# First token block in two halves, both gates on column tiles, and a rewritten order, in an adaLN block of windowed attention and a gMLP mixer

## The chip, the cores and the metric

The kernel runs on one core of one Trainium2 chip. The metric is the device time of one execution in microseconds, as the median of several runs. The engines are TensorE (PE), VectorE (DVE), ScalarE (ACT), GpSimd (POOL) and SyncE (SP), which only issues transfers. Each works through its own list of instructions in order, and waits on semaphores that the others raise.

## The reference

All is bfloat16: 2048 tokens of 448 features, 16 heads of 28, a causal window of 256 tokens, and a mixer of 2 x 896 hidden features that mixes over the 2048 tokens. `_layernorm` has no weights. The core of it:

```python
mod = (_silu(c) @ w_mod).reshape(c.shape[0], 6, 1, -1)
sa, ca, ga, sb, cb, gb = (mod[:, i] for i in range(6))
h = _layernorm(x) * (1 + ca) + sa
qkv = h @ wqkv                      # 16 heads of 28
scores = q k^T * 28 ** -0.5         # masked to 0 <= i - j < 256
x = x + ga * (softmax(scores) @ v) @ wo
h = _layernorm(x) * (1 + cb) + sb
z = gelu(h @ w_in)                  # 2 x 896
z1, z2 = z[..., :896], _layernorm(z[..., 896:])
g = w_sp @ z2 + b_sp                # over the 2048 tokens
x = x + gb * ((z1 * g) @ w_out)
```

## The kernel before

**Order by hand.** Nothing loops at run time. The kernel function adds some 1200 operations to a list (`sc.add`), each with the engines that could run it, its dependencies and the buffers it takes. The string ORDER (lines 19 to 74) then says in one sequence which operations run, on which engine and with which buffer slot: `671.v` is operation 671 on VectorE, `688.p.0` is operation 688 on TensorE with its first choice of PSUM banks (letters p, a, v, g, s for PE, ACT, DVE, POOL, SP). `Sched.order` (line 148) reads it, `waits` puts in the semaphore waits, `emit` writes out each engine's list. Operations that ORDER does not name are left out; `warm` (line 555) offers fillers that multiply the identity by itself, and ORDER takes 13 of them, all in the first 13 us. The durations written beside each operation were used in making ORDER; at run time they mean nothing.

**Head.** x's first 512 tokens come in two transfers of 256 tokens (`t_x0`, line 411), w_mod's first 896 columns in three pieces (`t_wmA`), the q and k columns of w_qkv in three each (`t_wq`). These are issued on SP and ACT, and x's next blocks, w_v, the rest of w_mod (`t_wmB`), w_o and w_in follow on SP. `mod_cols` (line 528) makes shift and scale of a layer norm as columns: for two vectors and four chunks of 128 features, four matmuls of one column each. The fourth chunk has 64 features; it is computed a second time into partitions 64 to 127 (line 540), because the transposed activations hold these features twice. `mod_out` brings them to `modT` in SBUF. The two gates ga and gb are rows: four matmuls each, with silu(c) repeated over 128 columns as the weights (line 570), one copy each to `gg_sb` (line 573). They scale w_o (`t_wog`, GpSimd) and w_out (`t_woutg`).

**Blocks of 512 tokens.** For each block `tb`, `stats` (line 589) takes mean and variance (VectorE) and the power -0.5 (GpSimd), `norm` writes the normalised tile `xn`. For blocks 0 and 1, PE transposes these (line 666) and the eviction applies scale and shift into `hT` (lines 678, 680); blocks 2 and 3 go through transposing transfers. Q and K of a block are eight groups of four matmuls with 512 columns. In block 0 the four groups of Q run chunk by chunk (line 696) so that they follow the evictions, then K (line 708). ScalarE or VectorE evict them to `qT` and `KT` (lines 718, 719); `q_dma` copies parts of Q to the block-diagonal `QBD`. V follows per tile (line 756).

**Attention.** Each of the 16 query tiles has two halves. A half is a score unit (32-row matmuls, line 832 or 858, and one full matmul, line 867), exponentials on ScalarE (line 819), masks on VectorE (line 874, or 894 for the first two tiles) and P times V (line 901). The score unit takes four fixed banks (0 to 3), so the next one waits for the exponential. Then a tile is divided by its sums, goes through a transposing transfer, the out-projection (line 926), the second layer norm, another transposing transfer, and the scale and shift (lines 949, 951).

**Mixer.** z2 is made per token tile (64-row matmuls, line 1011; Gelu on ScalarE, line 1018), normalised over its 896 features with two statistics and one aggregate on VectorE, the power on GpSimd and the final scaling on VectorE (line 1023). z1 is made feature by token in groups of four (line 1032). The spatial products (line 1055) are 28 groups of 16 matmuls of 512 columns, each needing all of z2; VectorE adds the bias (line 1059), GpSimd multiplies with z1 (line 1062), and four matmul groups per block give the output tiles (line 1072), with a sum (line 1082) and a store each.

Of the kernel before, what the change touches and what calls it, by code (L numbers as in the profile page):

```python
# [4 lines left out]
ACT = mybir.ActivationFunctionType  # L5
# [14 lines left out]
2.a 24.v 33.g 0.s 25.v 26.v 27.v 36.g 37.g 3.a 1.s 34.g 4.a 31.g 28.v 5.s 35.g 8.a 29.v 38.g 6.s 9.a 7.s 43.a 39.g 53.p.1 54.p.2 55.p.3 44.p.0 130.v  # L20
128.v 131.v 129.v 132.g 45.a 46.a 56.p.4 57.p.5 58.p.6 59.p.7 60.p.2 52.p.1 139.v 137.v 140.v 138.v 133.g 134.v 141.v 136.a.0 142.g 135.a.1 143.v
120.v 145.v.2 108.v 107.v 67.p.3 146.p.2 144.a.3 68.p.0 69.p.4 147.p 150.p.3 40.g 123.g 121.g 122.v 148.v 149.v 151.p 152.a 48.a 70.p.0 71.p.0
154.p.4.5.6.7 155.p 156.p 153.a 158.p 125.g 42.g 160.p 159.p 157.p 162.a 164.a 32.g 41.g 124.g 47.v 10.s 11.s 14.s 127.g 126.v 191.v 192.v 187.v 30.v
49.g 50.g 13.s 15.s 16.s 12.s 161.a 169.p.0 170.a 171.p.1 172.a 346.p.0 347.a.0 163.v 185.v 189.v 186.v 188.v 190.v 51.v 175.p.7 173.p.6 112.p.0
114.p.1 193.g 194.g 199.g 201.g 197.g 200.g.0 195.g 176.v 202.v.1 198.v.2 113.v 196.g.3 350.v 174.a 352.p.0 353.a.1 181.p.7 203.p.0 371.p.0 166.s
167.s 165.s 168.s 17.s 348.v 115.v 206.p.1 177.p.6 204.v 205.v 207.v 109.p.0 372.a.2 373.a 182.a 208.a 378.p.0 379.a.3 380.a 239.v 241.v 243.v 237.v
244.v 110.v 238.v 20.s 19.s 18.s 240.v 242.v 354.v 111.v 178.v 179.p.7 183.p.1 211.p.0 184.v 293.v 356.v 180.v 349.p.0 398.p.0 212.a 351.p 355.p
215.p.1 357.p 400.p.0 209.p.0 399.a.4.0 381.v 291.v 216.v 406.p.0 210.a 245.g 246.g 251.g 252.v.0 358.v 359.v.0 376.v 374.v 253.g 249.g 254.g.1 403.v
221.p.1 213.p.0 383.v 214.v 402.v 294.v 375.p.0 377.p 407.a.5.1 401.a 427.p.0 222.a 408.p.0 382.p 223.p.0 225.p.1 428.a.6.2 435.p.0 409.a 411.v
429.p.0 384.p 258.s 118.g 247.g 250.g.2 256.s 257.s 248.g.3 255.s 262.g 259.g 226.a 436.a.0.3 292.v 224.v 295.v 385.v 386.v.1 229.p.0 227.p.1 404.p.0  # L30
410.v 297.v 228.v 430.a 456.p.0 230.a 457.a.1.4 360.s 218.s 219.s 220.s 217.s 432.v 261.v 260.v 437.p.0 233.p.0 231.p.1 405.p 412.p 296.v 232.v 438.a
# [70 lines left out]
class Op:  # L102
    def __init__(self, n, ways, deps, prio, take, table, dma, lat, tail):
# [162 lines left out]
def bass_adaLN_cond__sliding_block__mixer_gmlp__prompt_kernel(  # L266
# [322 lines left out]
    def stats(slot, tiles, srcs, deps, prio, quick=False):  # L589
# [12 lines left out]
        if not quick:  # L602
            return rs
# [551 lines left out]
```

## Time and profile before

| what | value |
|---|---|
| median of 3 runs | 280.3 us (280.0 to 280.85) |
| the profiled execution, its own time | 279.08 us |
| its span, first to last instruction | 277.4 us |
| granted TensorE clock in the rows | 1.00 |
| first Q matmul (line 696) starts | 12.87 us |
| last z1 matmul before the spatial products | 156.5 us |
| last output matmul ends | 274.4 us |
| DMA issue to landing: x first half, second half | 3.9, 4.5 us |
| DMA issue to landing: w_mod's three first pieces | 4.4, 5.6, 5.8 us |
| DMA issue to landing: the two-chunk piece of w_q | 6.4 us |

The span is the window of one profiled execution; the time beside it also holds what lies around it. A row of the timeline gives start, length, engine, line, operation, and in square brackets how long the engine had been idle before it and what ended that. Successive instructions of one line are merged into one row (x15 is fifteen of them). A TensorE row's length includes the time in which its last matmul leaves the array, so the distance between starts says more about the rate than the length does. A few matmul records are missing.

### The profile page before, as it was taken

The numbers are of one execution on the slowest core, as the hardware profiler recorded it, in microseconds if no ns is written. First come the engines' busy times: TensorE is split into PE (matmuls) and PEld (weight loads), VectorE is DVE, ScalarE is ACT, GpSimd is POOL, SyncE is SP. The second block draws the span as 40 slices with busy tenths as digits, with TensorE's granted clock in tenths as the row PEclk, the third lists the DMA queues.
The fourth block names the chain that finished last, engine by engine and source line by source line (L and its number), as shares of the span: only waits on it lengthen the run. The fifth ranks groups of instructions, "written<-read, shape, count | busy, mean of one in ns | idle before, by whom it ended". The sixth has DMA issues, their size and how long they took to land.

```text
span 277.4 us, 7383 instructions
## 1 busy us (share of the span) xinstructions
PE 266.4 (96%) x3198; PEld 140.8 (51%) x3225; DVE 164.4 (59%) x364; ACT 128.2 (46%) x154; POOL 127.2 (46%) x191
## 2 busy tenths in 40 slices
PE   4999999999999999999999999999999999999995
PEld 1636466656576766444444444444444444444452
DVE  5679999989989999679798300300320042025434
ACT  2587999999999999577676600000000000000000
POOL 6831826914725669884949000600571065334110
PEclk9999999999999999999999999999999999999999
DMA  7966142145993666834999999100000000001113
GB/s 208 304 170 205 23 91 47 21 80 96 121 225 79 80 80 97 194 77 83 190 176 205 206 197 187 35 0 0 0 2 0 0 0 2 0 0 56 62 50 99
DMA packets 65843, 26.01 MB, mean 94 GB/s; under 512 B 56466, under 2 KB 64723, under 8 KB 65811
## 3 DMA queue, kind: packets, MB, share of 16 engines
q1 hardware_dynamic: 65168, 24.68, 43.4%
q10 hardware_dynamic: 642, 0.86, 1.1%
q8 instruction: 25, 0.41, 0.6%
q14 instruction: 8, 0.06, 0.1%
HBM read 9.01 MB, written 1.84 MB: 39 GB/s over the span
## 4 chain that ended last, share of the span: by engine, by line
PE 82%; DVE 8%; DMA 4%; POOL 3%; issue 1%; ACT 0%; ACTq 0%; SPq 0%; POOLq 0%
PE ps L1055 35%; PE ps L1032 8%; PE ps L1072 7%; PE ps L1011 6%; PE ps L708 5%; PE ps L901 5%; PE ps L858 3%; DMA hT<-xn 3%; PE ps L926 3%; PE ps L756 3%; PE ps L867 2%; DVE st_all L592 2%; PE ps L557 1%; DMA c_row<-in_c_dram 1%; PE ps L696 1%; POOL hT L951 1%
## 5 line engine op out<-in xcount | busy, mean ns | idle before, releaser
L819 ACT ACTIVATE PW<-ps 128x2048 bf16<-128x2048 f32 (+1 forms) x56 | 67.4, 1242 | 2.9 <-PE ps L867 1.1
L1059 DVE TENSOR_TENSOR tmpg<-ps,bsp_bc 128x512 bf16<-128x512 f32 x28 | 19.1, 691 | 83.4 <-PE ps L1055 69.3
L1062 POOL TENSOR_TENSOR z1T<-tmpg,z1T 128x512 bf16<-128x512 bf16 x28 | 31.9, 1153 | 79.3 <-DVE tmpg L1059 79.3
L1055 PE MATMUL ps<-wspB,z 128*128 128x512 bf16 x218 | 49.5, 379 | 0.3
L1055 PE MATMUL ps<-wspA,z 128*128 128x512 bf16 x220 | 48.8, 379 | 0.3 <-issue 0.2
L874 DVE TENSOR_TENSOR PT<-PW,mask 128x1024 bf16<-128x1024 bf16 x56 | 38.9, 721 | 0.7 <-ACT PW L819 0.7
L1055 PEld LDWEIGHTS ps<-wspA,z 128*128 128x128 bf16 x224 | 21.8, 98 | 26.6 <-issue 0.4
L1055 PEld LDWEIGHTS ps<-wspB,z 128*128 128x128 bf16 x224 | 21.9, 98 | 26.2
L600 POOL TENSOR_TENSOR rs_all<-ve_all,neghalf 128x1 f32<-128x1 f32 (+2 forms) x37 | 23.6, 645 | 3.7 <-DVE ve_all L597 3.0
L1011 PE MATMUL ps<-w_in,hT 64*128 64x448 bf16 x224 | 23.0, 349 | 1.2 <-DVE hT L951 0.6
L901 PE MATMUL ps<-Vaug,PT 128*128 128x32 bf16 x496 | 24.1, 177 | 0.1
L901 PEld LDWEIGHTS ps<-Vaug,PT 128*128 128x128 bf16 x496 | 21.8, 96 | 4.0 <-DVE PT L894 0.6
L1032 PE MATMUL ps<-hT,w_in 64*128 64x512 bf16 x196 | 22.5, 376 | 0.0
L1072 PE MATMUL ps<-w_out_g,z1T 128*128 128x448 bf16 x112 | 22.2, 352 | 0.0
L708 PE MATMUL ps<-hT,WQK 128*128 128x512 bf16 x80 | 20.5, 379 | 1.3 <-issue 0.4
L616 POOL TENSOR_SCALAR xn<-x_sb,rs_all,ve_all 128x448 bf16<-128x448 bf16 x21 | 18.1, 863 | 7.0 <-DMA hT<-xn 6.4
L901 PE MATMUL ps<-Vaug,PW 128*128 128x32 bf16 x224 | 20.1, 176 | 0.0
L592 DVE BATCH_NORM_STATS2 st_all<-x_sb 128x6 f32<-128x448 bf16 x32 | 18.9, 610 | 1.6 <-DMA x_sb<-in_A_x_dram 1.5
L592 DVE BATCH_NORM_STATS2 st_all<-z 128x6 f32<-128x448 bf16 x32 | 18.3, 607 | 1.7 <-ACT z L1018 1.7
L901 PEld LDWEIGHTS ps<-Vaug,PW 128*128 128x128 bf16 x224 | 17.6, 96 | 1.9
L597 POOL TENSOR_SCALAR ve_all<-mv_all 128x1 f32<-128x1 f32 (+2 forms) x20 | 6.6, 334 | 25.1 <-DVE mv_all L595 21.5
L1018 ACT ACTIVATE z<-ps 128x896 bf16<-128x896 f32 x16 | 14.1, 916 | 7.8 <-PE ps L1011 6.8
(101 smaller groups left out, 343.9 us busy)
## 6 DMA issues: line engine op xcount, KB each, us to landing
out_dram<-fin SPq DMA_DIRECT2D x16, 112.0 KB, 1.7
x_sb<-in_A_x_dram SPq DMA_DIRECT2D x3, 448.0 KB, 3.9
wmod<-in_w_mod_dram SPq DMA_DIRECT2D x1, 1344.0 KB, 9.5
w_in<-in_B_w_in_dram SPq DMA_DIRECT2D x1, 1344.0 KB, 8.2
QBD<-qT SPq DMA_DIRECT2D x16, 64.0 KB, 2.5
w_out_g<-in_B_w_out_dram SPq DMA_DIRECT2D x1, 784.0 KB, 4.9
bsp_bc<-in_B_b_sp_dram SPq DMA_DIRECT2D x1, 512.0 KB, 5.0
x_sb<-in_A_x_dram SPq DMA_DIRECT2D x2, 224.0 KB, 4.2
```

What stands on the lines that cost most here:

```text
L592: st = [dve(0.62 if True else 0, lambda e, t=t, ci=ci, s=s: e.bn_stats(st_all[:, slot, t, ci, :], s()), deps(t), prio) for ci, s in enumer ...
L600: rs = pool(0.53 + 0.15 * len(tiles), lambda e: e.tensor_tensor(rs_all[:, slot, a:b], ve_all[:, slot, a:b], neghalf[:, 0:b - a], ALU.pow), ...
L708: m = pe(4 * MMS, [lambda e, h=h, g=g, kc=kc, tb=tb: e.matmul(ps[:, h.slot[0], :], lhsT=WQK[:, kc, 4 * g:4 * g + 4, :].rearrange("p a b -> ...
L819: ex = act(xdur, lambda e, out_ap=out_ap, in_ap=in_ap: e.activation(out_ap(), in_ap(), ACT.Exp, scale=SCALE), [s], v - 8.0 + u, takes, tab ...
L874: return dve(0.70, lambda e: e.tensor_tensor(cols(hp.slot[0] * 2048 + 1024 * k, [[256, 4], [128, 2], [1, 128]]), cols(at_w() + 128 + 192 * ...
L901: fns.append(lambda e, hp=hp, hO=hO, hi=hi, bi=bi, kb=kb, hd=hd, nb=nb, a=at[hi][bi], p_of=p_of: e.matmul(ps[:, hO.slot[0], 32 * hd:32 * h ...
L1011: return lambda e, kc, p0, start, stop: e.matmul(ps[:, hs[t % 2].slot[hf], 0:D], lhsT=hT[p0:p0 + 64, kc, t * 128:(t + 1) * 128], rhs=w_in[ ...
L1032: return lambda e, kc, p0, start, stop: e.matmul(ps[:, hs[b // 2].slot[b % 2], :], lhsT=w_in[p0:p0 + 64, kc, ft * 128:(ft + 1) * 128], rhs ...
L1055: m = pe(16 * MMS, [lambda e, h=h, si=si, ft=ft, tb=tb: e.matmul(ps[:, h.slot[0], :], lhsT=z2[:, si, ft * 128:(ft + 1) * 128], rhs=(wspA i ...
L1059: a = dve(0.7, lambda e, h=h, ht=ht, tb=tb: e.tensor_tensor(tmpg[:, ht.slot[0], :], ps[:, h.slot[0], :], bsp_bc[:, tb * 512:(tb + 1) * 512 ...
L1062: u = pool(1.16, lambda e, ht=ht, ft=ft, tb=tb: e.tensor_tensor(z1T[tb][:, ft, :], tmpg[:, ht.slot[0], :], z1T[tb][:, ft, :], ALU.mult), [ ...
L1072: return [lambda e, ft=ft: e.matmul(ps[:, h.slot[0], 0:D], lhsT=z1T[t // 4][:, ft, (t % 4) * 128:(t % 4 + 1) * 128], rhs=w_out_g[:, ft, :] ...
```

## The change

**Block 0 in halves.** Transposes, evictions, Q and K of the first 512 tokens are made for tokens 0 to 255 and 256 to 511 separately: 8 evictions of 256 columns instead of 4 of 512, 64 matmuls of 256 columns instead of 32 of 512, 16 evictions of Q and K instead of 8. In the first half Q, then K, run chunk by chunk, each with the groups in pairs. Score units of the first tiles depend on the first half's Q (`QK_ready[...][0]`) and on K tile by tile.

**Loads.** ScalarE issues c and w_mod's large piece. SP issues x's first half, the two other pieces of w_mod, w_q's three, then x's second half, w_k's three, x's block 1. w_modB also waits for the first column matmuls.

**Columns and gates.** `mod_cols` computes the fourth chunk once with 128 columns instead of twice with 64; the 64 that spill over are zeros (`t_p2b`) for the first pair, and for the second pair one transfer (`d_modB`) copies partitions 0 to 63 of two columns of `modT` to 64 to 127, for which the columns are rotated by one. The gates are computed with 64-column weights, ga on partitions 0 to 63 and gb on 64 to 127 of one bank; one copy, then three transfers (`d_gg0`, `d_gg1`, `d_gg2`) spread each over 128 partitions.

**Normalisation.** `stats` now makes the shift (minus mean times power) for all its tiles in one operation, where `norm` had one GpSimd operation per tile. For the odd tiles of z2 (BY_ACT) the Gelu also sums its row, a Square on ScalarE gives the sum of squares, three small operations give variance and power. Tiles 0, 4, 8, 12 (BY_POOL) keep the statistics but are scaled on GpSimd.

**Output.** Tile 15 is made, summed and stored in two halves of 224 columns.

**ORDER** is new throughout. Decoded, what it says around these places:

- PE, head, before: 3 fillers, silu columns, 5 fillers, columns, filler, 4 transposes, 2 fillers, 12 transposes, 2 fillers, Q, two K groups, score unit 0.0, two K groups, gate 0, gate 1, score unit 0.1, V tile 2, ...
- PE, head, after: 2 fillers, silu columns, 5 fillers, columns, 8 transposes, 2 fillers, Q chunk 0, filler, rest of Q's first half, K's first half, 8 transposes, score unit 0.0, Q's second half, one K group, score unit 0.1, three K groups, score unit 1.0, gates, second columns, V tile 1, ...
- ACT, head, after: norm of tile 1, two evictions, pads of q and k, three Q evictions, norm of tile 3, three K evictions, one eviction of the second half, first exponential, three Q evictions, exponential.
- DVE, head, after: ... norm of tile 0, pad, clear of QBD, modT, two evictions, statistics of tiles 3 and 2, two pads, shift, norm of tile 2, one Q and one K eviction, three evictions of the second half, statistics of block 1.
- Out-projections start behind the score units of tile 9, before: of tile 6. 13 of h2's 16 scalings are on VectorE (before 4), 2 on ScalarE (5), 1 on GpSimd (7).
- POOL, end of z2, after: power of tile 15, power of tile 14, scaling of tile 0, shift, scaling of tile 12, scaling of tile 8, then the spatial products' multiplications. PE's list ends with the products of tiles 15 (halves), 12, 14, 13 and 1.

```diff
-    t_x0 = [load("d_x0%d" % i, "sp", 0.25, ..., prio=-98.99 + 0.001 * i, land=(2.9, 3.4)[i]) for i in range(2)]
+    t_x0 = [x_half("sp", 0, -98.99, 2.9, 2.9), x_half("sp", 1, -98.935, 8.0, 3.5)]
...
-    t_screp = dve(0.5, lambda e: e.tensor_copy(sc_rep[:], sc_sb[:].unsqueeze(2).broadcast_to([128, DC, 128])), [t_sc, t_x[1]], -16.0)
+    t_screp = dve(0.5, lambda e: e.tensor_copy(sc_rep[:], sc_sb[:].unsqueeze(2).broadcast_to([128, DC, 64])), [t_sc, t_x[1]], -16.0)
...
-                m = 128 if ch < 3 else 64
+                m = 128 if ch < 3 or not bank_col else 64
...
-    t_mA = pe(1.2, mod_cols(hA, (0, 1), True), [t_wmA, t_sc, t_p2], -60.0, [hA])
+    t_mA = pe(0.92, mod_cols(hA, (0, 1), False), [t_wmA, t_sc, t_p2, t_p2b], -60.0, [hA])
+    for d in t_wmB:
+        d.deps.add(t_mA)
...
+    t_modB.append(add({"sp": (0.6, lambda e: e.dma_start(modT[64:128, 11:13], modT[0:64, 11:13]))}, list(t_modB), -14.9, dma="d_modB", lat=0.05, tail=2.0))
+    hG = Hold(bM)
+    t_gate = pe(0.78, [lambda e, kc=kc, v=v, p0=p0: e.matmul(
+        ps[p0:p0 + 64, hG.slot[0], 0:D], lhsT=sc_rep[:, kc, :], rhs=wmod[:, kc, v * D:(v + 1) * D],
+        start=(kc == 0), stop=(kc == DC - 1), tile_position=(0, p0)) for kc in range(DC) for v, p0 in ((2, 0), (5, 64))],
+                [t_wmB, t_screp, t_p2], -14.0, [hG], "cols64")
+    t_graw = dve(0.7, lambda e: e.tensor_copy(gg_sb[:, 0, :], ps[:, hG.slot[0], 0:D]), [t_gate], -14.0)
...
+    t_gup = [spread("d_gg%d" % k, lambda p=p: gg_sb[p:p + 64, 1, :], lambda: gg_sb[64:128, 0, :], [t_graw]) for k, p in enumerate((0, 64))]
+    t_gg = [[t_graw, spread("d_gg2", lambda: gg_sb[64:128, 0, :], lambda: gg_sb[0:64, 0, :], [t_graw, t_gup])], t_gup]
...
+        by = lambda e: e.scalar_tensor_tensor(ve_all[:, slot, a:b], mv_all[:, slot, a:b, 0], -1.0, rs_all[:, slot, a:b], ALU.mult, ALU.mult)
...
-        nm = pool(0.34, lambda e: e.tensor_scalar(ve, m, z, -1.0, ALU.mult, ALU.mult), deps, prio)
...
+        for hf in range(2 if tb == 0 else 0):
+            xl = [xs[2 * hf], xs[2 * hf + 1]]
...
+                    four = range(4 * qk, 4 * qk + 4)
...
+                if hf == 0:
+                    for kc in range(DC - 1):
+                        for n in range(2):
+                            pair = four[2 * n:2 * n + 2]
...
+                        last[g] = pe(4 * MMH, [part(g, kc, hq[g], hf) for kc in range(DC)], [evh[hf], t_wqk[qk]], vv + 0.001 * g, [hq[g]])
...
+    BY_POOL = (0, 4, 8, 12)
+    BY_ACT = (1, 3, 5, 7, 9, 11, 13, 15)
...
+            g = act(1.1, lambda e, to=to, of=of, total=total: e.activation(to(), of(), ACT.Gelu_apprx_tanh, accum_out=total), need, v, table="gelu")
...
+            q = act(1.1, lambda e, t=t, less=less, square=square, hj=hj: e.activation(
+                fin[:, 2 * hj.slot[0]:2 * hj.slot[0] + 2, :].rearrange("p a d -> p (a d)"), z2[:, t, :], ACT.Square, bias=less, accum_out=square), [a], v, [hj])
...
+            r = pool(0.6, lambda e, t=t: e.tensor_tensor(rs_all[:, 2, t:t + 1], ve_all[:, 2, t:t + 1], neghalf[:, 0:1], ALU.pow), [b, t_nh], v - 0.01)
...
+            for c0, c1 in ((0, D // 2), (D // 2, D)) if t == NT - 1 else ((0, D),):
```

More of the change, by code (lines that the diff above doesn't have):

```diff
@@ L121, in __init__ @@
         self.land = None
+        self.least = 1.0
 class Sched:
@@ L179, in order @@
             if op.land is not None:
-                op.end = max(at + 1.0, op.land)
+                op.end = max(at + op.least, op.land)
                 dma_at = max(dma_at, op.end - 2.0)
```

356 lines of the change are left out of this document (214 added, 142 removed).

## The prediction

> **What bounds the kernel now.** I read the page first (shares of engines, then the chain of waits).
>
> ```profile
> span 277.4 us, 7383 instructions
> ...
> PE 266.4 (96%) x3198; PEld 140.8 (51%) x3225; DVE 164.4 (59%) x364; ACT 128.2 (46%) x154; POOL 127.2 (46%) x191
> ...
> PE 82%; DVE 8%; DMA 4%; POOL 3%; issue 1%; ACT 0%; ACTq 0%; SPq 0%; POOLq 0%
> ```
>
> TensorE is the bound: its work can only start earlier, shrink, or be stalled less. Each record holds some 0.17 us of pipeline, so I took the spacing of starts from the timeline: 512 columns cost 0.2156 us, 448 cost 0.189, 128 cost 0.056 (sixteen L743 matmuls in 0.89 us). Summing these over the matmuls and subtracting from the timeline leaves the true stalls: the head up to 12.87 us, 0.85 us at 18 us, about 1.1 us between 29 and 37 us, 1.75 us between 109 and 117 us. Almost none from 120 us to the last matmul at 274.4; then 2.95 us for the last sum and store. The head:
>
> ```profile
> 5.68 2.32 PE L557 MATMUL ps<-ident 128*128 128x512 bf16 x5
> ...
> 10.10 1.06 PE L557 MATMUL ps<-ident 128*128 128x512 bf16 x2
> 10.95 1.43 PE L666 MATMUL ps<-ident,xn 128*128 128x128 bf16 x12
> 12.22 0.59 PE L557 MATMUL ps<-ident 128*128 128x512 bf16 x2
> 12.87 3.40 PE L696 MATMUL ps<-hT,WQK 128*128 128x512 bf16 x15
> ...
> 18.68 0.29 PE L832 MATMUL ps<-qT,KT 32*128 32x128 bf16 x8 [0.69 <-ACT KT L718]
> ...
> 20.64 1.68 PE L570 MATMUL ps<-wmod,sc_rep 128*128 128x448 bf16 x8
> ```
>
> L557 only keeps the array busy; useful work starts at 12.87. The spacing matters too: two L557 from 10.10 to 10.95 are 0.43 us each and the transposes 0.107, twice the later figures, though PEclk reads 1.00. Full speed comes near 12.6 us, 3.4 us after the unbroken stretch that began at 9.27.
>
> Then windows, for the end of attention and what follows:
>
> ```profile
> 110.00:115.00 5.00, 4.61 (x58) 2.21 (x54) 3.08 (x9) 2.17 (x2) 4.12 (x9) 1.00 0.60 119
> 115.00:120.00 5.00, 4.44 (x48) 2.10 (x46) 4.58 (x12) 3.34 (x4) 4.24 (x9) 1.00 0.93 216
> 120.00:125.00 5.00, 5.00 (x48) 2.23 (x46) 3.62 (x12) 3.88 (x5) 4.01 (x9) 1.00 0.32 64
> ```
>
> (window, PE, PEld, DVE, ACT, POOL, clock, DMA.) The stall of 109 to 117 is here; VectorE and GpSimd are busy, ScalarE has room.
>
> **Part 1, the head.** I walked the new ORDER engine by engine with durations of this trace. x's first half keeps its issue, 0.79, and its landing 3.9 later: statistics from 4.76, two of 0.58, two aggregates 0.30, variance 0.17, GpSimd's power 0.73, shift 0.16, then two norms side by side (ScalarE 0.75): 8.2. w_mod landed at 7.6 (SP's third issue, 1.8, plus 5.8) behind all of x and beside w_q; now it is done with 1.0 MB moved instead of 1.23. x's second half landed at 5.8 with 0.93 MB moved, so between the two: estimate 6.2. Its 64 column matmuls, not 80, at 18 ns (80 took 1.44) end by 7.5. Eight transposes at 0.107 end at 9.1, two fillers at 9.97. VectorE meanwhile does a pad 0.28, the 0.91 clearing of QBD (L521), modT 0.30 and the first eviction 0.33 (from 0.54 for twice the columns): 9.7. So Q starts at 10.0, not 12.87.
>
> It does not keep those 2.9 us. Until about 11.65 (8.25 + 3.4) a 256-column matmul costs 0.213, then 0.109; with one filler of 0.43 Q ends at 12.8, K at 14.6. x's second half, moved behind w_q, has 1.62 MB ahead; w_q's large piece landed at 8.8 (2.4 + 6.4) with as much, so 8.8. VectorE takes it at 9.95: 1.16 + 0.30 + 0.17, GpSimd 0.73, and one norm at 12.9; but the other norm stands on ScalarE behind three Q evictions that need Q's last matmul (three of 0.39, estimated from L718's 0.60 and L819's 1.03 for 512 and 1024 columns): 14.75. Transposes to 15.25; ScalarE has three K evictions before its share of the next: 16.15. Second halves of Q and K, 32 x 0.109, and one score unit 0.25: 20.05. Score unit three needs the exponential of unit two, which follows a table load of 1.28: done at 20.75. Before, the same work ended at 20.65 plus two units of 0.22 still to come: 21.1. **Head: -0.35 us.** Its ends: -2.9 if nothing is late after the early start, +2.3 if the array stays slow one more 3.4 us stretch (rival 1).
>
> The issues: ScalarE's queue has two, not five, SP gets the rest, one per 0.5 to 0.6 us; the last w_k piece goes out near 6.6, not 4.8, but its turn by bytes is 10, and its pads are needed at 12.8. w_modB now waits for the first column matmuls, whose own load it already waited for: no later than 8.7.
>
> **Part 2, gates and columns.** Eight gate matmuls take 1.51 us (20.81 to 22.32). On two column tiles four pairs cost 4 x 0.189 = 0.76, plus a switch of shape, for which the nearest row is L832: eight 128-column matmuls on four row tiles should take 0.11 and take 0.23, so 0.12. **-0.63 us**; bounds +0.12 (pairs do not overlap) and -0.75. [...] The second set of columns loses 16 of 80 matmuls at 15 ns: **-0.24**.
> One copy of 0.62 remains of two on VectorE. Four new transfers (modT, three for gates) take 4 x 0.6 us on SP, which was idle from 22.8 to 31.2. They land 2.5 after issue (QBD's row), the last in a chain of two at about 28.4; the first reader, wo_g on GpSimd, started at 31.2. Without that cover GpSimd would stand there us for us, and block 3's norms behind it. x's last block, queued behind the wait for the gate copy, leaves at 23.4 instead of 22.3, lands by 28.7, and is read near 32.
>
> **Part 3, normalisation.** Twelve GpSimd shifts for blocks 1 to 3 (L614, 0.48 mean) become three VectorE ones of 0.16. Of z2's sixteen tiles, eight lose two statistics and an aggregate, 8 x 1.40 = 11.2 us of VectorE, and gain on ScalarE a Square and an accumulator each: 0.92 (L1018) to 1.2 (448 columns from SBUF take 0.75, scaled), some 8.5 us. ScalarE had 16 us idle from 110 to 157, so this hides, and is worth 8.5 us of PSUM waits if it did not. Four tiles' final scaling goes to GpSimd. With h2's scalings moved from GpSimd to VectorE and out-projections kept back as filler, I give back **1.0** of the 1.75 us stall (bounds -1.75, and +4.3, rival 2), and **0.5** of the 1.1 between 29 and 37 (0 to -1.1), where the first exponential is 2.5 us earlier.
>
> **Part 4, at nothing.** The last tile in halves: in the new ORDER tile 1, whole, is the last product, so the 2.95 us tail stays; were tile 15 last, half of 0.62 would go. 512 as 256-column matmuls: 32 more at 2.3 ns, 0.07. The shared shape of spatial products is untouched.
>
> **Sum**: -0.35 - 0.63 - 0.24 - 0.5 - 1.0 = -2.7. The profiled execution took 279.08 (span 277.4): 276.4. The median of three is 280.3, 1.2 above; the same step from it gives **277.6 us**.
>
> **Rivals.**
> 1. *The array stays slow.* PE pauses between the columns and the transposes (7.5 to 8.25) and there are three fewer fillers. If full speed came one stretch later, 16.0, Q and K's first halves would cost 32 x 0.213 + 0.43 = 7.3 us, ending at 17.2 instead of 14.6: +2.6, in all **280.2**, no change. [...] Against: from 8.25 the order is unbroken. [...]
> 2. *GpSimd holds the spatial products* (slower). They need all sixteen z2 tiles; GpSimd's queue ends with power, tile 0, a shift, tile 12, tile 8. After the last z2 matmul PE has four z1 groups, 112 x 0.108 = 12.1 us. ScalarE's last Square ends some 5 us in, small operations take 2, leaving 5.1 for three scalings. The row below (L951's) is 512 columns at 0.76 to 1.79; 896 columns are 1.33 to 3.14, three 4.0 to 9.4. At the slow end PE stands 4.3 us: **281.9**. It delays from 1.7 each and makes the kernel slower from 2.9 each. For: GpSimd slows beside a busy VectorE. Against: the median is 767.
>
> ```profile
> L951 POOL TENSOR_SCALAR hT<-hT,modT x7: 762/767/1793, 100.4 to 131.6; 128x512 bf16<-128x512 bf16 x7
> ```
>
> 3. *The early start carries through.* -2.9, both stalls fully gone (-2.85) and part 2: -6.6, **273.7**. For: ScalarE and TensorE both get the score chain sooner. Against: the walk above ends at ScalarE.
> 4. *Halves do not pay at all* (x's second half lands near 11): head +1.1, rest as forecast: 279.0, inside the forecast's range.
>
> **Chances.** Forecast with 4: 0.57; rival 1: 0.13; rival 2: 0.13; rival 3: 0.17. About 0.3%, 279.5 to 281.1, is what a measurement of this kernel can tell from no change. Faster 0.73 (forecast but 0.03, rival 3, a little of rival 1), same 0.12, slower 0.15 (rival 2, and rival 1 with one more stall). The range 274.2 to 280.8 leaves out rival 2 and rival 3's end; the forecast alone is 275.8 to 279.4.
>
> **What would show it.** First useful Q matmul near 10 us; QK's last near 20; the gate's eight matmuls within 0.9 us; spacing 0.213 then 0.109 inside Q's first half; the wait of ScalarE's second norm on PE; no PE gap before the first spatial product; gaps of 109 to 117 halved. Wrong: QK still ending after 21, or a PE gap over 1 us near 152.

## The result and the profile after

The changed kernel takes 280.94 us (median of 20 executions, 280.01 to 282.97); the kernel before, on the same chip, 279.95 (20 executions, 278.2 to 282.4). The ratio is 1.0055, 95% interval 1.0034 to 1.0076: about half a per cent **slower**, where 277.6 and "faster" had been forecast, and just above the range. The profiled execution has a span of 279.0 us against 277.4.

From the page of the changed kernel, the lines that answer to those shown of before, and the row of the granted clock over the 40 slices:

```profile
span 279.0 us, 7462 instructions
...
PE 266.4 (96%) x3222; PEld 143.8 (52%) x3245; DVE 160.2 (57%) x373; ACT 133.0 (48%) x179; POOL 117.1 (42%) x174
...
PEclk9999999999999999979999999999999999999999
...
PE 71%; POOL 13%; DVE 8%; issue 4%; DMA 2%; ACT 0%; SPq 0%; POOLq 0%
```

TensorE's busy time has not changed by a tenth; VectorE and GpSimd do less, ScalarE more. GpSimd has gone from 3% to 13% of the chain that ends last, DMA stands at 2%, and one slice of the clock, the 18th (119 to 126 us), reads 7.

TensorE's timeline at the head:

```profile
8.71 1.06 PE L747 MATMUL ps<-hT,WQK 128*128 128x256 bf16 x4
9.57 0.63 PE L569 MATMUL ps<-ident 128*128 128x512 bf16 x1
9.99 3.27 PE L747 MATMUL ps<-hT,WQK 128*128 128x256 bf16 x28
...
14.95 2.36 PE L747 MATMUL ps<-hT,WQK 128*128 128x256 bf16 x20 [0.65 <-DVE hT L708]
...
18.88 0.40 PE L907 MATMUL ps<-qT,KT 32*128 32x128 bf16 x16
19.21 0.95 PE L582 MATMUL ps<-wmod,sc_rep 128*64 128x448 bf16 x8
20.09 0.95 PE L544 MATMUL ps<-sc_sb,wmod 128*128 128x1 bf16 x32
20.91 0.92 PE L831 MATMUL ps<-wv,hT 128*128 128x448 bf16 x4
```

The head is better than forecast. Q starts at 8.71 us, Q, K and three score units of the first block are done at 19.2, the gates take 0.88 us from start to start. The same work, counted as in the prediction, ended in the kernel before at 21.1, and with gates and second columns at about 23.8: a lead of 1.9 us, then of 2.9. This is one execution. In the eleven profiled executions with this order of loads (the changed kernel and all runs below but e7 and e8) the gates start between 19.2 and 20.3 us, so a lead read from one profile is uncertain by about a microsecond.

The loss is behind 105 us. TensorE there, and the same stretch in windows of one us (PE, PEld, DVE, ACT, POOL, clock, DMA):

```profile
107.18 1.69 PE L1089 MATMUL ps<-w_in,hT 64*128 64x448 bf16 x16 [0.29 <-DVE st_all L612]
...
112.36 2.82 PE L1089 MATMUL ps<-w_in,hT 64*128 64x448 bf16 x28
115.47 0.92 PE L1001 MATMUL ps<-wo_g,hT 128*128 128x448 bf16 x4 [0.28 <-DMA hT<-o_sb]
118.37 0.93 PE L1001 MATMUL ps<-wo_g,hT 128*128 128x448 bf16 x4 [1.99 <-DMA hT<-o_sb]
119.24 7.15 PE L1089 MATMUL ps<-w_in,hT 64*128 64x448 bf16 x56
...
158.29 4.05 PE L1158 MATMUL ps<-wspA,z 128*128 128x512 bf16 x18 [0.16 <-issue]
```

```profile
119.00:120.00 1.00, 1.00 (x8) 0.34 (x8) 1.00 (x3) 0.84 (x2) 0.30 (x1) 0.65 0.21 29
120.00:121.00 1.00, 1.00 (x8) 0.39 (x6) 0.97 (x2) 0.00 (x0) 0.85 (x3) 0.50 0.64 148
121.00:122.00 1.00, 1.00 (x8) 0.46 (x6) 0.96 (x5) 0.67 (x1) 0.42 (x3) 0.50 1.07 369
122.00:123.00 1.00, 1.00 (x8) 0.41 (x6) 0.96 (x4) 0.46 (x2) 0.38 (x2) 0.64 1.22 344
123.00:124.00 1.00, 1.00 (x14) 0.53 (x12) 0.88 (x3) 0.00 (x0) 0.90 (x2) 1.00 1.39 210
```

The output product of block 15 (omm.j15, 118.37) waits 1.99 us for its transposed attention output, and behind this pause 8 matmuls a microsecond run instead of 14: 3.4 us (0.7 x 1, 2 x 1, 0.7 x 1) at half the clock, worth some 1.7 us. TensorE is never idle in the windows from 119 to 123; "PE 1.00" hides the loss, and only the clock column and the counts show it.

Why the transposed rows are late is seen on SP's queue, which issues the transposes in order, and on GpSimd:

```profile
105.64 1.26 SPq L475 DMA_TRANSPOSE hT<-o_sb  x1
109.39 3.41 SPq L475 DMA_TRANSPOSE hT<-xn  x2
112.84 1.27 SPq L475 DMA_TRANSPOSE hT<-o_sb  x1
114.57 1.19 SPq L475 DMA_TRANSPOSE hT<-xn  x1
115.82 1.25 SPq L475 DMA_TRANSPOSE hT<-o_sb  x1
```

```profile
107.31 1.86 POOL L637 TENSOR_SCALAR xn<-x_sb,rs_all,ve_all 128x448 bf16<-128x448 bf16 x1
...
112.80 0.71 POOL L637 TENSOR_SCALAR xn<-x_sb,rs_all,ve_all 128x448 bf16<-128x448 bf16 x1 [2.21 <-DMA hT<-xn]
```

Block 14's attention output was ready at 106, but its transpose (112.84) stands behind those of h2 blocks 5 and 4 (109.39), which waited for a GpSimd norm that took 1.86 us (107.31) where its shortest took 0.71. From 106.9 to 109.4 SP issues nothing; then five transposes of 1.2 to 1.7 us each are due at nearly the same time, and block 15's is the last of them.

How much this stage costs can be summed. Its two ends in the kernel before:

```profile
109.32 2.25 PE L1011 MATMUL ps<-w_in,hT 64*128 64x448 bf16 x22 [0.29 <-ACT PW L819]
...
156.59 3.62 PE L1055 MATMUL ps<-wspA,z 128*128 128x512 bf16 x16 [0.16 <-issue]
```

From the first z2 matmul to the first spatial product TensorE has 224 x 0.0945 + 196 x 0.108 + 4 x 0.756 + 0.6 (the last PV) = 46.0 us of work (45.2 in the kernel before, where one output product is already done). It took 51.1 us (107.18 to 158.29) against 47.3 (109.32 to 156.59): **5.1 us lost, where 2.1 were lost before**. Of the 3.0 us between them, 1.3 are longer waits (0.28 and 1.99, against 0.40 and 0.56) and 1.7 are the half clock. At the stage's start the lead is still 1.3 us; 1.6 of the 2.9 had gone on the way. Two of the waits on the way are large, and the second is taken up by e4:

```profile
38.85 0.19 PE L976 MATMUL ps<-Vaug,PT 128*128 128x32 bf16 x1 [0.59 <-DVE o_sb L992]
...
46.82 0.81 PE L789 MATMUL ps<-hT,WQK 128*128 128x512 bf16 x3 [1.32 <-DVE Vaug L836]
```

### The profile page after: what moved, and what is told of

It reads as the page before. It is cut to its first block, busy times and chain, and to the rows that moved or that the text cites. A ratio compares the mean times of both kernels' runs of the same rounds, so it can differ in the third digit from the quotient of the medians.

```text
span 279.0 us, 7462 instructions
## 1 busy us (share of the span) xinstructions
PE 266.4 (96%) x3222; PEld 143.8 (52%) x3245; DVE 160.2 (57%) x373; ACT 133.0 (48%) x179; POOL 117.1 (42%) x174
## 4 chain that ended last, share of the span: by engine, by line
PE 71%; POOL 13%; DVE 8%; issue 4%; DMA 2%; ACT 0%; SPq 0%; POOLq 0%
PE ps L1158 34%; PE ps L1177 8%; PE ps L1135 8%; PE ps L1089 6%; POOL xn L637 5%; PE ps L789 4%; POOL rs_all L620 3%; PE ps L976 2%; PE ps L831 2%; PE ps L933 2%; POOL ve_all L627 1%; PE ps L747 1%; DVE PT L949 1%; DVE st_all L612 1%; DMA hT<-xn 1%
## 5 line engine op out<-in xcount | busy, mean ns | idle before, releaser
L949 DVE TENSOR_TENSOR PT<-PW,mask 128x1024 bf16<-128x1024 bf16 x56 | 37.9, 709 | 1.7 <-ACT PW L894 1.7
L620 POOL TENSOR_TENSOR rs_all<-ve_all,neghalf 128x1 f32<-128x1 f32 (+2 forms) x29 | 19.4, 672 | 12.3 <-DVE ve_all L617 7.0
L1089 PE MATMUL ps<-w_in,hT 64*128 64x448 bf16 x224 | 23.9, 368 | 0.3 <-DVE st_all L612 0.3
L637 POOL TENSOR_SCALAR xn<-x_sb,rs_all,ve_all 128x448 bf16<-128x448 bf16 x22 | 20.6, 939 | 5.5 <-DMA hT<-xn 3.7
L617 POOL TENSOR_SCALAR ve_all<-mv_all 128x1 f32<-128x1 f32 (+1 forms) x16 | 4.7, 295 | 42.4 <-DVE mv_all L615 41.3
L1177 PE MATMUL ps<-w_out_g,z1T 128*128 128x448 bf16 (+1 forms) x119 | 22.0, 341 | 0.0
L1135 PE MATMUL ps<-hT,w_in 64*128 64x512 bf16 x196 | 21.6, 376 | 0.0
L789 PE MATMUL ps<-hT,WQK 128*128 128x512 bf16 x68 | 17.8, 379 | 2.1 <-DVE Vaug L836 1.3
L1187 DVE TENSOR_TENSOR fin<-ps,x_sb 128x448 bf16<-128x448 f32 (+1 forms) x17 | 9.8, 593 | 14.9 <-PE ps L1177 14.8
L1089 PEld LDWEIGHTS ps<-w_in,hT 64*128 64x128 bf16 x224 | 11.2, 98 | 11.9 <-issue 2.3
```

The source lines that it names most:

```text
L620: rs = pool(0.53 + 0.15 * len(tiles), lambda e: e.tensor_tensor(rs_all[:, slot, a:b], ve_all[:, slot, a:b], neghalf[:, 0:b - a], ALU.pow), ...
L637: op = add({"dve": (0.42, on_dve), "pool": (0.75, lambda e: e.tensor_scalar(to[:, h.slot[0], 0:D], x_sb[:, t, :], z, ve, ALU.mult, ALU.add ...
L789: m = pe(4 * MMS, [lambda e, h=h, g=g, kc=kc, tb=tb: e.matmul(ps[:, h.slot[0], :], lhsT=WQK[:, kc, 4 * g:4 * g + 4, :].rearrange("p a b -> ...
L949: return dve(0.70, lambda e: e.tensor_tensor(cols(hp.slot[0] * 2048 + 1024 * k, [[256, 4], [128, 2], [1, 128]]), cols(at_w() + 128 + 192 * ...
L1089: return lambda e, kc, p0, start, stop: e.matmul(ps[:, hs[t % 2].slot[hf], 0:D], lhsT=hT[p0:p0 + 64, kc, t * 128:(t + 1) * 128], rhs=w_in[ ...
L1135: return lambda e, kc, p0, start, stop: e.matmul(ps[:, hs[b // 2].slot[b % 2], :], lhsT=w_in[p0:p0 + 64, kc, ft * 128:(ft + 1) * 128], rhs ...
```

## The experiments

Kernels are compared by their ratio to the kernel before, timed on the same chip beside them. "Lost" is the excess over 46.0 us (45.2 for "before" and e7, which have the old order) in the profiled execution, as above; "half rate" counts the timed executions whose mean granted clock was 0.994 or less (one stretch of 3.4 us at half rate lowers the mean of 279 us by 0.006); "pause" is TensorE's longest recorded wait of the profiled execution between 107 and 135 us. The pause belongs to one execution of each kernel, the half rate to all of them.

| kernel | ratio [95%] | lost, us | pause, us | half rate |
|---|---|---|---|---|
| before | 1 | 2.1 | 0.56 | 6 of 105 |
| changed | 1.0055 [1.0034, 1.0076] | 5.1 | 1.99 | 17 of 20 |
| e1_oT_first | 1.0051 [1.0019, 1.0084] | 3.0 | 1.90 | 9 of 12 |
| e2_fill_gap | 1.0005 [0.9977, 1.0033] | 3.8 | 0.41 and fillers | 0 of 12 |
| e4_h1_gpsimd | 1.0021 [0.9994, 1.0048] | 3.5 | 2.26 | 6 of 12 |
| e5_ready_work | 0.9991 [0.9961, 1.0021] | 3.4 | 1.77 | 2 of 12 |
| e6_ready_h1 | 1.0022 [0.9989, 1.0055] | 3.7 | 1.77 | 0 of 12 |
| e7_pause_before | 1.0028 [0.9998, 1.0057] | 1.4 | 0.58 | 1 of 12 |
| e8_x_whole | 1.0096 [1.0061, 1.0131] | 5.7 | 2.74 | 6 of 6 |
| e9_five_xn | 1.0065 [1.0041, 1.0089] | 5.4 | 2.28 | 9 of 12 |
| e12_all_four | 0.9986 [0.9962, 1.0010] | 2.6 | 1.06 | 3 of 12 |
| e13_all_five | 0.9979 [0.9959, 0.9999] | 3.1 | 1.06 | 2 of 12 |
| e14_gates_row | 1.0064 [1.0042, 1.0086] | 5.1 | 2.01 | 7 of 11 |
| e15_all_six | 0.9943 [0.9919, 0.9966] | 1.4 | 0.34 | 0 of 8 |

In the diffs a line of ORDER is written with the names of its operations, one engine at a time.

**e1_oT_first.** The two late transposes move forward in SP's queue: block 14's ahead of those of h2 blocks 5 and 4, block 15's ahead of block 4's.

```diff
 SP:
-oT.j13 h2T.j5 h2T.j4 oT.j14 h2T.j6 oT.j15 h2T.j8
+oT.j13 oT.j14 h2T.j5 oT.j15 h2T.j4 h2T.j6 h2T.j8
```

> The changed kernel with SyncE's queue alone reordered: the transposing transfers of attention tiles 14 and 15 go ahead of second-norm transfers that wait for GpSimd. My theory (late transfers stop TensorE for 2.3 us near 116 us, and the pause halves its rate from 119.3 to 122.6 us, another 1.65 us): both out-projections find their tile, no gap over 0.5 us there, clock 1.00 throughout, 3 to 4 us less than the changed kernel, so about 277 us, 0.985 to 0.993 of before. Rival A (the head start was used up before 107 us and the pause only shows it; the work behind it waits anyway, for the second norms): the gap moves behind the out-projections, less than 1 us won.

The output products run without a wait, and TensorE then stands for h2 instead:

```profile
115.20 1.69 PE L1001 MATMUL ps<-wo_g,hT 128*128 128x448 bf16 x8
118.79 5.54 PE L1089 MATMUL ps<-w_in,hT 64*128 64x448 bf16 x56 [1.90 <-DVE hT L1026]
```

The wait has changed its name and kept its place and length. In this run SP's order decides which of the transposes is late, not that one is. The profiled execution happens to be one without half rate (span 276.9); 9 of the 12 timed ones have it, some of them twice, and the median does not gain, where 3 to 4 us had been expected. One profile would have told the wrong story here.

**e2_fill_gap.** Ten more of the matmuls that only keep the array busy (L569) ahead of omm.j15.

```diff
 PE:
-omm.j14 omm.j15
+omm.j14 warm40.3 warm40.4 warm40.5 warm40.6 warm40.7 warm40.8 warm40.9 warm40.10 warm40.11 warm40.12 omm.j15
```

> The changed kernel with ten identity matmuls of 512 columns (2.16 us) on TensorE between the last two out-projections; the transfer is as late as before. My theory (the half rate comes from the pause): clock 1.00 throughout, the pause is filled but not shortened, 1.3 to 1.8 us less than the changed kernel. Rival B (the half rate is not tied to the pause): a stretch of half rate remains and the time is equal or up to 0.5 us longer.

No execution of the 12 is at half rate any more, and the ratio falls from 1.0055 to 1.0005: some 1.4 us (0.4 to 2.4 by the two intervals) for matmuls that compute nothing, while omm.j15 comes no earlier (119.88). So the half-rate stretch is caused by TensorE standing still there, and is about 1.4 us of the loss; the waiting itself is still there, as filler.

**e4_h1_gpsimd.** Aims at the wait of 1.32 us ahead of 46.82, where four modulations of h1 in a row on VectorE stand before a V eviction, while GpSimd is idle.

```diff
 GpSimd:
-wog2 wog0 rs0.t12
+wog2 wog0 h1mod.b2.ch2 h1mod.b2.ch3 rs0.t12
 VectorE:
-h1mod.b2.ch2 h1mod.b2.ch3
```

> The changed kernel with two of the four scalings of block 2 moved from VectorE, where all four ran from 43.6 to 46.0 us, to GpSimd, idle from 36.2 to 41.5 us. My theory (the head start of 2.9 us at 21 us is partly lost because VectorE is late at 45 us): the TensorE gap of 1.3 us near 45 us shrinks below 0.5, but the time changes by less than 0.7 us, since the pause at 116 us is set by GpSimd and SyncE. Rival A (everything before 107 us counts): about 1 us less than the changed kernel.

The wait falls to 0.36, with another of 0.20 just ahead of it. How much of this arrives at 107 us can be read by the distance from the first gate matmul to the first z2 matmul, which leaves out how late the head was: 87.97 us in the changed kernel and 88.06 to 88.17 in the six other runs of the changed kernel without this edit (e1, e2, e5, e8, e9, e14), 87.37 here and 87.36 to 87.58 in the four others that have it (e6, e12, e13, e15). So some 0.6 us of the 1.6 lost between 21 and 107 come back. What that is worth at the end is not shown: the ratio 1.0021 is lower than the changed kernel's, but the intervals overlap, and half rate is also rarer here (6 of 12).

**e8_x_whole.** Undoes the move of x's second half.

```diff
 SP:
-ld x0.0 ld wmAb ld wmAc ld wqb ld wqa ld wqc ld x0.1
+ld x0.0 ld x0.1 ld wmAb ld wmAc ld wqb ld wqa ld wqc
```

> The changed kernel with the second half of x's first 512 tokens loaded right behind the first half again, ahead of the w_mod and w_q loads; nothing is left out. It undoes the part of the head that my prediction put at 0.35 us. Theory A (the start of the Q products is set by w_mod's and w_q's arrival, which the second half of x delays): the first Q matmul comes 0.7 to 1.0 us later than 8.7, the lead over the kernel before at the end of the first block's K products falls by as much, and as the pause near 116 us follows the rest of the kernel, the time is 281.3 to 282. Rival (the pause near 116 us is set by transfers and norms that do not follow the head): the time stays at 280.9, only the pause gets shorter.

Q starts at 9.69 instead of 8.71, the gates at 21.23 instead of 19.21, the first z2 matmul at 109.40 instead of 107.18, and the ratio is 1.0096, 0.41% or 1.1 us above the changed kernel; with six executions and overlapping intervals, that size is uncertain by about as much. The gates come 0.9 to 2.0 us later than in the eleven executions of the other order (19.2 to 20.3). A late head is carried through attention: its sixteen blocks, under one order, come later by what the head is late (the reciprocals of blocks 0 to 15 stand 2.0 to 2.2 us later throughout).

**e14_gates_row.** Four gate matmuls of one column tile, then four of the other.

```diff
-        start=(kc == 0), stop=(kc == DC - 1), tile_position=(0, p0)) for kc in range(DC) for v, p0 in ((2, 0), (5, 64))],
+        start=(kc == 0), stop=(kc == DC - 1), tile_position=(0, p0)) for v, p0 in ((2, 0), (5, 64)) for kc in range(DC)],
```

> The changed kernel with the eight gate matmuls in the order of the two gates, four of one column tile and then four of the other, instead of turn by turn; nothing is left out. It undoes the overlap of the two column tiles, which my prediction put at 0.63 us. If the two tiles run side by side only when they alternate, the eight take 1.5 us instead of 0.8 at 19.2 us, and what is lost at the head reaches the end as with e8_x_whole (1.2 us for 2 us): 281.2 to 281.7. Rival (two tiles overlap in any order, or the loss is covered behind 21 us): 280.9 as before.

```profile
19.70 0.96 PE L582 MATMUL ps<-wmod,sc_rep 128*64 128x448 bf16 x8
20.59 0.95 PE L544 MATMUL ps<-sc_sb,wmod 128*128 128x1 bf16 x32
```

0.89 us from start to start against 0.88: the order of the two tiles does not matter, and the time is the changed kernel's within the intervals. The overlap of the two tiles stayed, so this run does not show what the gates are worth at the end.

**e7_pause_before.** Meant to build the pause into the kernel before. (A first form of this, e3_before_late_oT, with block 15's transpose moved three places back on SP, gave no time.)

```diff
 SP:
-oT.j15 h2T.j10 h2T.j11 h2T.j8
+h2T.j10 h2T.j11 oT.j15 h2T.j8
 PE:
-z2mm.t4.3 z1mm.1.0 omm.j15
+z2mm.t4.3 omm.j15 z1mm.1.0
```

> The kernel BEFORE with the pause built in: on SP's queue the transposes h2T.j10 and h2T.j11 ahead of oT.j15, and on TensorE omm.j15 ahead of z1mm.1.0 instead of behind it; nothing is left out. Theory A (a pause of about 2 us in a full-rate stretch is enough for a half-rate stretch behind it, whatever the head does): oT.j15 is issued near 120.5 us and lands near 123, TensorE pauses about 2 us ahead of omm.j15 near 121, most executions show a mean granted clock of 0.994 or less, and the time rises by 2 us of pause and about 1 us of half rate, to 282.5 to 284. Rival (the half rate belongs to the changed kernel, to its column tiles or its denser start, not to the pause): the clock stays at 1.000 and only the pause is paid, 281.5 to 282.5.

The pause did not come: the whole of attention ran later in the profiled execution, and omm.j15 waited 0.58 us. So it does not test what it was for. But that execution is one of the few of the old order at 0.994, and its trace shows where:

```profile
72.39 0.38 PE L867 MATMUL ps<-QBD,KT 128*128 128x512 bf16 x1 [1.08 <-DMA QBD<-qT]
...
72.91 2.95 PE L756 MATMUL ps<-wv,hT 128*128 128x448 bf16 x8
```

```profile
73.00:74.00 1.00, 1.00 (x7) 0.40 (x4) 0.90 (x3) 0.00 (x0) 0.72 (x1) 0.57 0.52 65
74.00:75.00 1.00, 1.00 (x4) 0.38 (x3) 0.45 (x2) 0.59 (x2) 0.00 (x0) 0.50 0.93 234
75.00:76.00 1.00, 1.00 (x15) 0.27 (x17) 0.10 (x1) 0.44 (x1) 0.00 (x0) 0.50 2.42 91
76.00:77.00 1.00, 1.00 (x39) 0.66 (x32) 1.00 (x5) 0.35 (x1) 0.00 (x0) 0.72 0.21 14
```

A late transfer of QBD leaves TensorE idle for 1.08 us, and from 73.1 to 76.6 us 3.4 us at half rate follow. It needs neither the change's order nor its column tiles.

**e9_five_xn.** GpSimd's wait of 2.21 us at 112.80 is for a buffer: three hold the second norm's rows, and each is free only when its transpose has landed. Here there are five, taken in turn.

```diff
-    xn2, xn2_off, _ = alloc("xn2", [128, 3, DP], BF16)
+    xn2, xn2_off, _ = alloc("xn2", [128, 5, DP], BF16)
-    x2R = Res(range(3), [(i,) for i in range(3)])
+    x2R = Res(range(5), [(i,) for i in range(5)])
```

> The changed kernel with five buffers for the second norm's rows (xn2) instead of three, taken in turn; no instruction moves and nothing is left out. Theory A (the stage behind 105 us is a ring: GpSimd's norm waits for a buffer, the buffer for its transpose, the transpose for its place in SP's queue): GpSimd's waits for a transpose at 112.8, 117.3 and 119.7 us (2.2, 0.25 and 1.2 us) go, and the h2 of blocks 8 to 11 comes some 2 us earlier; but oT.j14 still stands behind h2T.j5 and h2T.j4 on SP, so the pause near 116 us stays at 1.5 to 2 us, and the time falls by less than 0.5 us: 280.4 to 280.9. Rival (the buffers are the bound of the whole stage, the pause too): 278.5 to 279.5, clock 1.000.

GpSimd's waits for buffers shrink from three (3.7 us) to one of 1.14, and the pause stays, 2.28 us. The buffers are not what makes the pause; that rival falls.

**e5_ready_work.** Puts useful work that is ready, a group of value products on h2 of blocks 0 to 3, into the pause, as the kernel before had it; the PSUM banks of the products behind it change with the order.

```diff
 PE:
-omm.j14 omm.j15 z2mm.t6.. z2mm.t4.. z1mm.1.. z1mm.0.. z2mm.t10.0 z2mm.t8.0
+omm.j14 z1mm.0.. omm.j15 z2mm.t6.. z2mm.t4.. z1mm.1.. z2mm.t8.0 z2mm.t10.0
 ScalarE:
-z2gelu.t3 z2sq.t3 z2gelu.t4
+z2gelu.t3 z1gelu.b0.f0 z1gelu.b0.f1 z1gelu.b0.f2 z1gelu.b0.f3 z2sq.t3 z2gelu.t4
```

> The changed kernel with the first group of value products, z1mm.0 (28 matmuls that need only the first four blocks' h2), between the output products of blocks 14 and 15, the eight z2 products of blocks 4 to 7 after it, and its four Gelus ahead of z2gelu.t4; nothing is left out. Theory A (the time is lost where TensorE pauses near 116 us, in two parts: the pause of 2.0 to 2.3 us itself and, in most executions, about 3.3 us at half rate behind it): the pause falls under 0.5 us, no execution shows a mean granted clock of 0.994 or less, and the time falls by 2 to 3 us from the changed kernel's 280.9, to 278 to 279. Theory B (only the half rate costs; what pauses is on a chain of norms and transfers that sets the end by itself): as with the ten filler matmuls, 280.2, with the pause turning up again at the next z2 products. Theory C (the lead is lost somewhere behind 126 us): 280.9 as before.

Theory B came true in its time (0.9991) and in the place where the wait turns up again; its reason, a chain of norms and transfers, did not hold, as e6 and e12 show. The pause at 116 is gone (0.25), and 1.77 us come back at 131.6, at the z2 products of blocks 8 to 11. **e6_ready_h1** adds e4's edit.

> The kernel of e5_ready_work with two of the four first-block-2 modulations (chunks 2 and 3 of h1mod of tokens 1024 to 1535) moved from VectorE to GpSimd, as in e4_h1_gpsimd; nothing is left out. Theory A: the 1.48 us pause at 45 us falls to about 0.5, and since the pause near 116 us is now covered, that microsecond reaches the end: 0.5 to 1 us below e5_ready_work, 277.3 to 278.3. Theory B: no gain over e5_ready_work, since the norms near 107 us, not TensorE, set the time there.

The first z2 matmul comes 1.6 us earlier than in e5 (0.9 of it is the earlier head of that execution, 0.7 e4's edit), and the end is no better (1.0022, an interval that holds 1 and e5's ratio): what is gained ahead stops at the same wait. VectorE's timeline in e6 says whose it is:

```profile
127.75 0.15 DVE L1116 TENSOR_SCALAR mv_all<-st_all 128x1 f32<-128x1 f32 x1 [1.99 <-ACT z L1112]
...
128.44 0.40 DVE L1026 TENSOR_SCALAR hT<-hT,modT 128x512 bf16<-128x512 bf16 x1
```

VectorE stands 1.99 us in front of a 0.15 us mean of tile 5 (z2mean.t5), which needs ScalarE's Gelu of that tile, now the last of four; h2's modulations, which TensorE waits for, stand behind it. With that mean moved behind them (e12), this wait is gone.

**e12_all_four, e13_all_five, e15_all_six.** e12 is e6 with e1's SP order and with z2mean.t5 behind those modulations; e13 adds the five buffers; e15 lets the next z2 products take the PSUM banks that come free first.

```diff
 VectorE (e12):
-z2mean.t5 xnc1.t13 bn2.t0.1 h2mod.b2.ch2 xn1.t14 ag2.t0 h2mod.b2.ch0 h2mod.b2.ch1 xnc1.t14 h2mod.b2.ch3
+xnc1.t13 bn2.t0.1 h2mod.b2.ch2 xn1.t14 ag2.t0 h2mod.b2.ch0 h2mod.b2.ch1 xnc1.t14 h2mod.b2.ch3 z2mean.t5
 ScalarE (e15):
-z1gelu.b0.f5 z1gelu.b0.f6 z2sq.t5 z1gelu.b0.f4 z1gelu.b1.f0
+z1gelu.b0.f4 z1gelu.b0.f5 z1gelu.b0.f6 z1gelu.b1.f0 z2sq.t5
```

> e6_ready_h1 with two more moves, nothing left out: on SP oT.j14 and oT.j15 ahead of h2T.j5 and h2T.j4 (as in e1_oT_first), and on VectorE z2mean.t5, which waited 2.0 us for ScalarE's eighth Gelu, behind the four h2mod of blocks 8 to 11 that stood behind it. Theory A (what is left in e6_ready_h1 is the pause of 1.77 us at 128 us, and that is VectorE's order): the pause at 128 us falls under 0.7 us, those near 116 stay under 0.7, no half rate: 277.3 to 278.3 with the kernel before at 279.8. Rival (the ring of norms, buffers and transposes sets the end): the pause turns up at the next z2 products and the time stays at 279 to 279.6.

> e12_all_four with five buffers for the second norm's rows instead of three; nothing left out. Theory A: 0 to 0.4 us below e12_all_four. Rival (the ring): 1 us or more below it, 277.5 to 278.3.

> e13_all_five with the pair of PSUM banks of the z2 products of blocks 9 and 11 exchanged and ScalarE's four value Gelus of that group ahead of z2sq.t5, so that the ninth block's z2 products take the banks that come free first; nothing left out. Theory A (TensorE's wait of 1.06 us for a value Gelu at 131 us, the last pause over 0.5 us behind 107 us, is on the path to the end): the wait goes, the time falls by 0.5 to 1 us below e13_all_five, to 0.993 to 0.996 of the kernel before. Rival (behind it the next norms or Gelus are as late): the wait moves on by one group, 0.997 to 0.999.

e12 comes to 0.9986, where 0.991 to 0.995 had been expected, and e13 to 0.9979. Each still has a wait of 1.06 us near 131, for a value Gelu; in e12:

```profile
131.64 2.63 PE L1089 MATMUL ps<-w_in,hT 64*128 64x448 bf16 x26 [1.06 <-ACT z1T L1143]
```

That they beat the changed kernel is plain; that the buffers add anything is not (the intervals overlap). In e15 the last wait is gone:

```profile
113.10 2.82 PE L1089 MATMUL ps<-w_in,hT 64*128 64x448 bf16 x28
115.85 0.93 PE L1001 MATMUL ps<-wo_g,hT 128*128 128x448 bf16 x4
116.71 3.20 PE L1135 MATMUL ps<-hT,w_in 64*128 64x512 bf16 x28
119.84 0.93 PE L1001 MATMUL ps<-wo_g,hT 128*128 128x448 bf16 x4
120.88 5.68 PE L1089 MATMUL ps<-w_in,hT 64*128 64x448 bf16 x56
126.40 3.19 PE L1135 MATMUL ps<-hT,w_in 64*128 64x512 bf16 x28
129.54 5.47 PE L1089 MATMUL ps<-w_in,hT 64*128 64x448 bf16 x56
```

No line ends in a wait. The stage loses 1.4 us, no execution is at half rate, and the kernel takes 277.81 us (277.43 to 278.80, 8 executions) against 279.41 of the kernel before: **0.9943, faster than both kernels**. It does all of the change; what differs is only the order behind 30 us, two operations moved to GpSimd, the PSUM banks of some products and two more buffers. Of the runs only this one, with all the edits together, is plainly faster than the kernel before (e13's interval ends at 0.9999); which of them could be left out, no run shows.

## Why the prediction was wrong

The sum had five terms. Three were right in sign, and together larger than forecast; two had the wrong sign, and they decide.

- **Part 1, the head, -0.35: mechanism right, size wrong.** The lead is 1.9 us at 19.2 in this execution, 0.8 to 1.9 in the eleven (against the one trace of the kernel before). The first mis-sized term is the landing of x's first half, kept at 3.9 us: VectorE takes it at 3.60 without a wait, so it landed at most 2.8 us after its issue. Its statistics start there, not at 4.76, so Q starts at 8.71, not 10.0; K's first half ends at 13.3, not 14.6; and the second half's transposes start at 13.29, not 14.75. Of the waits I had named, the one for the second half's norm does not show; 0.65 for its modulation does, a microsecond or more earlier than forecast. Full rate came at 9.99 in this execution (0.215 spacing before it, 0.11 after), not at 11.65 and not one stretch later, so rival 1 did not happen. The 8.25 + 3.4 behind 11.65 was my estimate from one stretch of the kernel before (9.27 to 12.6), though rows of TensorE run without a recorded wait from 5.38 there, and no run shows it to hold: here full rate comes 2.95 us behind the first transpose (7.04), and in e6 and e14 the transposes at 7.34 and 7.69 have it already (0.056 and 0.055 each).
- **Part 2, -0.63 and -0.24: right.** Gates 0.88 us instead of 1.51; with the columns the lead grows from 1.9 to 2.9, so that 0.37 is left for them.
- **Part 3, "0.5 of the 1.1 between 29 and 37": wrong sign.** TensorE waits 0.59 us at 38 for an attention output on VectorE and 1.32 at 45 for a V eviction behind four modulations. Between 21 and 107 us the lead falls from 2.9 to 1.3; e4 shows that the second of these waits is the order's, and that some 0.6 us can be had back. The rest was not tried.
- **Part 3, "I give back 1.0 of the 1.75 us stall": the step that failed.** The stage lost 5.1 us instead of 2.1, so the term was +3.0, not -1.0; it lies within the bound (+4.3) that I had written beside it and then put at GpSimd's last operations. With the terms as they turned out, -1.9 - 0.63 - 0.37 + 1.6 + 3.0 = +1.7, the span's +1.6.

Neither sign that I had named for being wrong appeared (QK ended at 19.2, no gap near 152); what failed is "gaps of 109 to 117 halved".

The step counted on the out-projections that the new order keeps back as filler. They were no filler, because they were not ready: omm.j14 and omm.j15 are the products that wait for their transposes (0.28 and 1.99 us). What the step left out is of two kinds. First, I argued from the busy shares of engines (VectorE and GpSimd full, ScalarE with room) and walked ScalarE's, VectorE's and GpSimd's order at the head, but never SP's order behind 105 us: oT.j14 behind two transposes whose rows a GpSimd norm delivers last. And the new order finishes attention earlier (block 15's reciprocal at 109.6, not 113.9) and keeps its z1 products for later, so where the old order had z1 work in front of omm.j15, the new one has nothing that is ready. e5 shows that this work, put back in its place, removes the wait there, and e15 that the time falls below both kernels once the next two waits go as well. Second, a pause has a price beyond its length: half the clock for 3.4 us in 17 of 20 executions, about 1.4 us by e2.

Rival 2 (GpSimd ahead of the spatial products) did not come: the first spatial product starts after 0.16 us of issue. A slow GpSimd norm does matter, but some 50 us earlier, as the one that holds SP's queue back at 107 to 109 us. Rival 3's condition, an early start that carries, is seen within attention (e8) and, in part, at the end of e15.

What stays open: e15 still gives back part of its lead between 21 and 107 us, and no run separates what the halved x, the gates and the columns are each worth at the end in a kernel without the pause.

## What to carry to other kernels

A gain at the head is worth what the first stage with little ready work lets through: sum that stage's matmuls and compare with its length, before and after, and walk the in-order queue that feeds it, the DMA issuer's too. When a wait is removed and the time stands still, look for a wait of like length under another name downstream (here omm.j15, then h2 of blocks 4 to 7, then 8 to 11, then a PSUM bank), and remove the row of them before judging the idea. Read the clock of every execution beside its time: a profile may be the one execution without the loss.

## What the runs showed of the hardware

**Behind a pause of about 2 us most executions ran some 3.4 us at half rate.** Kernels whose profiled execution shows a pause of 1.9 to 2.3 us had a mean clock of 0.994 or less in 48 of 67 executions (changed, e1, e4, e9, e14), with 2.74 us (e8) in 6 of 6, with 1.77 as the longest (e5, e6) in 2 of 24, with 1.06 (e12, e13) in 5 of 24, and e15, without one, in 0 of 8. The changed order without e4's edit also waits 1.3 us at 45, and e2, where that is the longest, shows none. Where the stretch lies is seen in the profiled executions alone: in the changed kernel, e8, e9 and e14 it begins between 0.2 us before and 1.5 us behind the pause's end, and in e7 behind a pause of only 1.08 us. In the changed kernel it is 3.4 us long (119.3 to 122.7). Much the same pause sometimes costs nothing (1.90 us in e1's profiled execution, 2.26 in e4's, both at clock 1.00 throughout).

**The order of the matmuls of two column tiles did not matter**: eight in 0.88 us taking turns, 0.89 four and four.

**A VectorE norm of 0.40 us took 1.69** (11.46 us, while GpSimd cleared a buffer), and GpSimd norms of 0.71 took up to 2.11. The slow one of 1.86 at 107.31, while VectorE was masking (L949), set SP's queue back at 109 us. In the kernel before, a GpSimd modulation (L951) took 1.79 us at 106.67, where VectorE ran two masks (L874, 106.69 to 107.98), against a median of 0.77; the one ahead of it, beside a division on VectorE (L917, 106.15), was over in 0.75 to 0.77. That the other engine is the cause was not tested.

**ScalarE's sums along a row are an instruction of their own**, 0.18 to 0.24 us behind each Gelu and Square that has one; sixteen of them are 3.3 us of ScalarE beside 8.4 for the eight Squares. Part 3's 8.5 us fits the Squares alone. ScalarE had the room in the changed kernel, where it has no share of the chain that ended last (ACT 0%); in e12 and e13 the last wait is for one of its Gelus.
